# Splitting each weight's conversion around the H block of a slot

## The chip, the cores and the metric

The kernel runs on one core of a Trainium2 chip. The metric is the device time in microseconds of one execution. TensorE is called PE below, VectorE DVE, ScalarE ACT, GpSimd POOL and the queue that issues the transfers SP.

## The reference

Three computations follow each other:

```python
# attention: batch 4, 12 heads, 448 tokens, head size 64, causal
scores = q @ k.T / 8;  attn = exp(masked scores - row maximum);  attn /= row sum
x = (attn @ v) as [1792, 768]
# MLP: w_in [768, 2048], w_out [2048, 768], drawn as 64-bit floats
h = x @ w_in;  g = max(0.01 * h, h);  x = g @ w_out
# soft mixture: phi [768, 32], 8 experts of 4 slots, w1 [8, 768, 1024], w2 [8, 1024, 768]
logits = x @ phi;  d = softmax(logits, over tokens);  c = softmax(logits, over slots)
slot_input = d.T @ x;  slot_out[e] = max(slot_input[e] @ w1[e], 0) @ w2[e];  out = c @ slot_out
```

## The kernel before

**Attention** goes by pairs of heads: 24 pairs n, six to a batch. A pair takes three slots, which we call A, B and C after the first six pairs: A has the products of the probabilities of pair n-1 with v (tile `O`), their row sums (`dn`) and the transposed maxima (`mps`, copied to `mr`); B has score products of pair n+1 (`S`, for the row maxima on DVE, tiles `junk` and `mxe`), the transposed scores `T` of pair n for its first key block, and once more `S`; C has the two further `T`, one more `S` and the transposes of q and k (`qkps`, copied to `qkt` on ACT in line 349 and DVE in line 350). ACT makes the probabilities `P` of each `T` by an exponential (L408). The tiles `S` and `T` share two PSUM buffers in turn: the second `S` of B waits for the maxima of the first, and the `S` of C waits for the exponential of the first `T` of C. On DVE the reciprocals of the row sums (L450, after ACT's copy in L448) and the scaling of `O` (L483) stand in the same queue as the maxima.

**The MLP's first product** of batch b runs in the slots of batch b+1: one H block per slot, 18 products of 448 columns for 128 columns of w_in, evicted by ACT (L668, tile `g`). There are 18 slots to a stage and 16 blocks; the slots 6 and 15 have none. There is one PSUM buffer for H.

**The weights** come as 64-bit floats and are converted in the same slots, in units of 128 columns of w_in (`i`) or 128 rows of w_out (`o`, whole, or in two halves from o10 on). A unit's elementwise passes are: ACT takes magnitude and sign (L200, L201), DVE the unit's maximum (L203, w_in only) and the two passes that put the 32-bit float together (L204, L205), after which the next raw tile can be loaded. For w_in, a TensorE product (`w_ps`) and a chain of small DVE operations (L116 to L124) make a power-of-two scale `w_s` of the maximum; then ACT scales the sign (L221), POOL multiplies (L222), ACT makes the high half (L228) and POOL the low half (L229). For w_out, POOL multiplies (L238), and the products `wt_ps`, `wp_ps`, `wf_ps` with their copies on ACT (L253, L262, L266) fold it with phi. Units i0 to i5 are done during the first batch's attention, i6 to i15 in the slots of pairs 7 to 12, o0 to o9 in those of pairs 13 to 18, o10 to o15 in those of pairs 19 to 23.

**Order.** Each engine runs its queue in order. A scheduler sets the queues when the program is built, from the order in which the code emits the work and the data's dependences; what stands under `tc.high_priority` (attention and H blocks) is ranked as if it had been emitted 300 places earlier. Each unit is a generator whose `yield`s divide it into steps, and `prep_step` advances every running unit by one step per slot, behind attention and block.

Of the kernel before, what the change touches and what calls it, by code (L numbers as in the profile page):

```python
# [10 lines left out]
F32 = mybir.dt.float32  # L11
# [14 lines left out]
AHEAD = 300  # L26
EARLY = (6, 10, 10)


def as_float(bits):  # L30
    return struct.unpack("<f", struct.pack("<I", bits))[0]
# [3 lines left out]
def tile_attn_moe_softmoe(ctx: ExitStack, tc: tile.TileContext, q, k, v, w_in, w_out, phi, w1, w2, out, dbg=None):  # L35
    nc = tc.nc
# [6 lines left out]
    E, _, FE = w1.shape  # L43
# [3 lines left out]
    NP = H // 2  # L47
    NF = DFF // 128
# [9 lines left out]
    ident = const.tile([128, 128], F32, name="ident")  # L58
# [29 lines left out]
    def ps_tr(name, shape=(128, 512)):  # L88
        return psum.tile(list(shape), F32, tag="tr", bufs=TR[0], name=name)
# [16 lines left out]
    tr = partial(in_order, nc.tensor.transpose)  # L106


    def pow2_scale(absmax, name, shift=23, bias=0, out=None):


        ps = ps_tr(f"{name}_ps", (128, 128))
        op = nc.tensor.matmul if name == "v0" else mm
        op(ps, absmax.to_broadcast([128, 128]), ident, start=True, stop=True)
        m1 = const.tile([128, 1], F32, tag="p2_m1", bufs=2, name=f"{name}_m1")
        nc.vector.tensor_reduce(m1, ps, AX.X, ALU.max)  # L116
        nc.vector.tensor_scalar(m1, m1, as_float((27 + bias) << shift), None, ALU.max)
        e = const.tile([128, 1], I32, tag="p2_e", bufs=2, name=f"{name}_e")
        nc.vector.tensor_scalar(e, m1.bitcast(I32), shift, None, ALU.logical_shift_right)
        si = const.tile([128, 2], I32, tag="p2_s" + name[0], bufs=4, name=f"{name}_s")  # L120
        nc.vector.tensor_scalar(si[:, 0:1], e, -(2**23), (268 + bias) * 2**23, ALU.mult, ALU.add)
        if out is None:
            out = si[:, 1:2].bitcast(F32)
        nc.vector.tensor_scalar(out.bitcast(I32), e, 2**23, -(14 + bias) * 2**23, ALU.mult, ALU.add)  # L124
        return si.bitcast(F32)[:, 0:1], out
# [23 lines left out]
    for x, u in enumerate(units):  # L149
        stage = 0 if x < EARLY[0] else 1 if x < whole else 2  # L150
        order += [u + (h, stage) for h in ((0, 1) if stage == 2 else (None,))]
    waiting = list(order)
    pools = [None, None, None]
# [58 lines left out]
    def prep_in(u):  # L212

        f = u[1]
        am = const.tile([128, 1], F32, tag="w_am", bufs=2, name=f"w_am{f}")
        t, sg = to_f32(u, am)
        yield
        if f >= EARLY[0]:
            yield
        s_w, _ = pow2_scale(am, f"w{f}", 20, out=inv_w[:, f : f + 1])  # L220
        nc.scalar.activation(sg, sg, AF.Copy, scale=s_w)  # L221
        nc.gpsimd.tensor_tensor(t, t, sg, ALU.mult)  # L222
        w = t.rearrange("p (c f) -> p c f", c=NP)
        hi, lo = (w16[f // 4][:, x, :, 128 * (f % 4) : 128 * (f % 4 + 1)] for x in range(2))
        if f < EARLY[0] and f % 4 < HIP:
            nc.gpsimd.tensor_copy(hi, w)
        else:
            nc.scalar.copy(hi, w)  # L228
        nc.gpsimd.tensor_tensor(lo, w, hi, ALU.subtract)  # L229
        ready.add(u[:2])  # L230

    def prep_out(us):

        f, stage = us[0][1], us[0][3]
        wt = None
        for u in us:
            wo, sg = to_f32(u)
            nc.gpsimd.tensor_tensor(wo, wo, sg, ALU.mult)  # L238
            c0 = DH * (u[2] or 0)
            nc.sync.dma_start(  # L240
                wsc.rearrange("(k g a p) n -> k a g p n", k=4, g=4, a=4)[f // 4, f % 4][:, :, c0 : c0 + wo.shape[1]], wo
            )
            yield
            if u[2] is None:
                yield
            if wt is None:
                wt = pools[stage].tile([128, NP, 128], F32, tag="wt", bufs=1, name=f"wt{f}")
            for h in (0, 1) if u[2] is None else (u[2],):
                ps = ps_tr(f"wt_ps{f}_{h}", (128, 3, 128))
                for j in range(3):  # L250
                    c = 128 * (3 * h + j) - c0
                    tr(ps[:, j], wo[:, c : c + 128], ident)
                nc.scalar.copy(wt[:, 3 * h : 3 * h + 3], ps)  # L253
        yield
        psw = ps_tr(f"wp_ps{f}", (96, 128))
        for c in range(NP):
            j = c % 3
            mm(
                psw[32 * j : 32 * j + 32], phi_sb[:, c], wt[:, c], start=c < 3, stop=c >= 3, skip_group_check=True
            )  # L260
        w4 = pools[stage].tile([96, 128], F32, tag="w4", bufs=1, name=f"w4_{f}")
        nc.scalar.copy(w4, psw)  # L262
        yield
        psf = ps_tr(f"wf_ps{f}", (128, NS))
        mm(psf, w4, istack[:96, :NS], start=True, stop=True)
        nc.scalar.copy(wprime[:, f], psf)  # L266
        ready.add(us[0][:2])

    ready = set()

    started = [0]
    running = []

    def prep_step():

        for g in list(running):
            if next(g, 1) == 1:
                running.remove(g)

    def prep_start():  # L280
        u = units[started[0]]
        started[0] += 1
        us = [x for x in order if x[:2] == u]
        g = prep_in(us[0]) if u[0] == "i" else prep_out(us)
        next(g)
        running.append(g)

    def need(u):
        while u not in ready:
            if not running:  # L290
                prep_start()
            prep_step()

# [330 lines left out]
    def up(b, before=()):  # L626
# [14 lines left out]
        for f in range(NF):  # L641
            if b == 0:
                need(("i", f))
                scales(slice(f, f + 1))
# [134 lines left out]
    def stage(slots, count, columns_of_g=None):  # L779

        had = started[0]
        for x in range(slots):
            with tc.high_priority(offset=AHEAD):
                next(slots_of_attention, None)
                if columns_of_g is not None and x not in GAPS:
                    next(columns_of_g)
            prep_step()
            while started[0] < min(count, had + -(-(count - had) * (x + 1) // (slots - (4 if columns_of_g is None or count > NF else 6)))):
                prep_start()
        if columns_of_g is not None:  # L790
            with tc.high_priority(offset=AHEAD):
                for _ in columns_of_g:
                    pass
        while running:
            prep_step()

    if True:
        pools[0] = tc.alloc_tile_pool(name="conv1", bufs=1)
# [31 lines left out]
        slots = ["wg"] * (NG - 1) + ["wq"] * NQ + ["wx"] * NX + ["wg"] + ["wc"] * NC  # L830
# [78 lines left out]
        for c in range(4):  # L909
            wo = loaded.pop(("wo", c))  # L910
# [23 lines left out]
        for e in range(E):  # L934
            ph = ps2(f"ph{e}", (128, 256), tag="h", bufs=4)
            for hf in range(2):
                wt = loaded.pop(("w1", (e, hf)))
# [83 lines left out]
        for x, (t0, nt, c0, cols) in enumerate(pieces):  # L1021
            if x:
                load_next(1)
            wt = loaded.pop(("w2", x))
            hp = padded_h(t0 // 8)
            for h in (0, 1) if cols == DM else (c0 // DH,):
                for t in range(nt):
                    g = (t0 + t) % 4
# [19 lines left out]
GAPS = (6, 15)  # L1048
# [34 lines left out]
```

## Time and profile before

| | |
|---|---|
| median of 3 runs | 712.88 us (705.38, 712.88, 713.38) |
| the profiled execution | 705.66 us, of which the span of its instructions 703.9 us |
| PE busy | 592.6 us, 84% of the span |
| DVE, ACT, POOL busy | 358.0, 289.7, 236.6 us |
| mean granted TensorE clock | 0.951 |

The slots that the change touches lie between about 110 and 475 us of the span: the first H blocks run at 114 us, the third stage ends at about 475 us. Behind that the last batch's MLP follows, and then the experts' weights, which the transfers set. Times in the rows are microseconds from the span's start. An "idle before" of an engine is followed by what the profile takes as its releaser.

### The profile page before, as it was taken

Reading aid. Unit: us, or ns where it says so; the run is one execution under the profiler, and the core shown is the slowest. Engines: PE = TensorE matmul, PEld = TensorE weight load, DVE = VectorE, ACT = ScalarE, POOL = GpSimd, SP = SyncE. Lnnn points to the kernel's source line nnn. Section 1 sums busy time; section 2 is a strip of 40 time slices with the busy share of each in tenths; the row PEclk is TensorE's granted clock in tenths of the full one; section 3 lists DMA queues with packets and bytes.
Section 4 is the critical chain, followed back from the end, with each engine's and each line's share of the span. In section 5 each row is a group of like instructions: output and inputs, shape, how many; then the busy total and the mean of one; then the engine's idle time right before and its main releaser. Section 6 shows DMA issues by size and latency. Waiting matters only on the chain.

```text
span 703.9 us, 12298 instructions
## 1 busy us (share of the span) xinstructions
PE 592.6 (84%) x4836; PEld 334.8 (48%) x4836; DVE 358.0 (51%) x884; ACT 289.7 (41%) x571; POOL 236.6 (34%) x247
## 2 busy tenths in 40 slices
PE   3788868877989999899988979999997996998644
PEld 2555544544555555465555545554343443453114
DVE  5868646775764564654645655644555423001004
ACT  1577543656565356465444455442022112011013
POOL 4277743675586342553522434440000000000000
PEclk9999998997989999999999999999999997899798
DMA  9932352542643246663313422206979335999967
GB/s 182 270 99 49 70 173 54 169 129 85 167 145 109 66 150 170 178 189 112 97 49 111 109 81 64 79 24 230 303 279 406 107 146 219 426 423 425 423 259 313
DMA packets 102449, 125.67 MB, mean 179 GB/s; under 512 B 69240, under 2 KB 91256, under 8 KB 98296
## 3 DMA queue, kind: packets, MB, share of 16 engines
q1 hardware_dynamic: 102392, 124.89, 54.2%
q8 instruction: 38, 0.62, 0.4%
q14 instruction: 19, 0.16, 0.1%
HBM read 105.74 MB, written 19.14 MB: 177 GB/s over the span
## 4 chain that ended last, share of the span: by engine, by line
PE 48%; DMA 13%; DVE 11%; ACT 10%; POOL 8%; issue 7%; SPq 1%; ACTq 0%; DVEq 0%; POOLq 0%
PE H L102 22%; DMA w<-in_moe_w_dram 8%; PE O L102 5%; PE g_acc L102 3%; DVE g_nat L608 2%; DVE rs L450 2%; PE S L102 2%; ACT P L408 2%; PE qkps L102 2%; POOL cv_i_None L222 2%; PE ph L941 2%; DMA raw_i_None<-in_moe_w_in_dram 2%; PE dn L102 2%; PE L L102 2%; PE T L102 2%
## 5 line engine op out<-in xcount | busy, mean ns | idle before, releaser
L102 PE MATMUL H<-x,w 128*128 128x448 f16 x1152 | 234.8, 359 | 0.7 <-ACT g L668 0.7
L102 PEld LDWEIGHTS <-w 128*128 128x128 f16 x1152 | 112.5, 100 | 113.4 <-issue 22.5
L372 DVE CUSTOM_DVE_ANT_0 junk<-S,mask 112x224 bf16<-112x224 f32 (+3 forms) x192 | 85.1, 443 | 47.8 <-PE S L102 44.7
L668 ACT ACTIVATE g<-H,iv 128x448 f32<-128x448 f32 x58 | 36.7, 633 | 112.1 <-PE H L102 101.3
L450 DVE RECIPROCAL rs<-rs 128x224 f32<-128x224 f32 x36 | 53.4, 1524 | 38.2 <-ACT rs L448 38.2
L102 PE MATMUL S<-qkt 64*112 64x224 f32 (+3 forms) x192 | 33.8, 393 | 35.0 <-ACT P L408 21.8
L102 PE MATMUL O<-P,v 112*64 112x448 f32 (+3 forms) x384 | 57.4, 444 | 6.1 <-POOL P L412 4.4
L102 PE MATMUL T<-qkt 64*112 64x336 f32 (+3 forms) x576 | 58.4, 315 | 3.9 <-ACT P L408 3.2
L412 POOL TENSOR_SCALAR_AFFINE_SELECT P<-P 112x448 f32<-112x448 f32 x48 | 33.8, 708 | 82.1 <-ACT P L408 69.3
L408 ACT ACTIVATE P<-T 112x672 f32<-112x672 f32 (+1 forms) x72 | 55.8, 791 | 12.1 <-PE T L102 11.8
L485 POOL TENSOR_TENSOR x<-rs,x 128x448 f16<-128x448 f32 x24 | 25.3, 1053 | 84.9 <-ACT x L484 79.6
L102 PEld LDWEIGHTS T<-qkt 64*112 64x112 f32 x576 | 43.1, 180 | 10.4 <-ACT P L408 3.6
L421 POOL TENSOR_TENSOR tsum<-tsum,P 112x448 f32<-112x448 f32 (+1 forms) x48 | 46.4, 967 | 3.1
L102 PEld LDWEIGHTS O<-P,v 112*64 112x64 f32 x384 | 27.5, 148 | 35.2 <-issue 17.6
L1029 PE MATMUL po<-w,hz 128*32 128x384 f32 x256 | 27.3, 548 | 17.7 <-DMA w<-in_moe_w_dram 17.7
L417 POOL TENSOR_TENSOR tsum<-P 112x672 f32<-112x672 f32 x24 | 39.4, 1643 | 1.3
L102 PEld LDWEIGHTS S<-qkt 64*112 64x112 f32 x192 | 16.0, 184 | 50.1 <-ACT P L408 25.6
L933 POOL MEMSET hz<- 128x256 f32 x2 | 0.6, 312 | 109.6 <-PE g_acc L102 109.6
L608 DVE STREAM_TRANSPOSE g_nat<-g 128x448 f32<-128x448 f32 x26 | 16.5, 640 | 37.7 <-ACT g L668 37.7
L350 DVE TENSOR_TENSOR qkt<-qkps,qkt 128x448 fp32r<-128x448 f32 x48 | 28.9, 620 | 10.5 <-ACT qkt L349 10.5
L222 POOL TENSOR_TENSOR cv_i_None<-cv_i_None,cs_i_None 128x768 f32<-128x768 f32 x16 | 28.0, 1747 | 16.8 <-ACT cs_i_None L221 16.8
L384 ACT ACTIVATE mr<-mps,own 128x112 fp32r<-128x112 f32 x96 | 26.2, 361 | 16.0 <-PE mps L102 16.0
(174 smaller groups left out, 865.8 us busy)
## 6 DMA issues: line engine op xcount, KB each, us to landing
w<-in_moe_w_dram SPq DMA_DIRECT2D x32, 1536.0 KB, 20.8
raw_i_None<-in_moe_w_in_dram SPq DMA_DIRECT2D x16, 768.0 KB, 4.6
raw_o_None<-in_moe_w_out_dram SPq DMA_DIRECT2D x10, 768.0 KB, 6.0
g_far<-g SPq DMA_DIRECT2D x32, 224.0 KB, 6.4
gb<-g_far SPq DMA_DIRECT2D x8, 896.0 KB, 6.7
wo<-wsc SPq DMA_DIRECT2D x4, 1536.0 KB, 10.0
qk<-in_q_dram SPq DMA_DIRECT2D x48, 112.0 KB, 2.5
qk<-in_k_dram SPq DMA_DIRECT2D x48, 112.0 KB, 2.9
```

Of the source, the lines that this page charges most:

```text
L102: op(*args, **kwargs)
L222: nc.gpsimd.tensor_tensor(t, t, sg, ALU.mult)
L350: nc.vector.tensor_tensor(st[:, j, 1], p, st[:, j, 0].bitcast(F32), ALU.subtract)
L372: nc.vector.tensor_tensor_reduce(out=junk[:, :w], in0=ps[:, a, at : at + w], in1=mask[:, S - w :], scale=-1.0, scalar=3e38, op0=ALU.add, o ...
L408: nc.scalar.activation(x[:, :, o : o + at], ps[:, :, :at], AF.Exp, scale=SCALE)
L412: nc.gpsimd.affine_select(out=d, in_=d, compare_op=ALU.is_ge, fill=0.0, base=0, pattern=[[0, 4], [1, CP]], channel_multiplier=-1,)
L417: nc.gpsimd.tensor_tensor(tsum[:CP], p[0][:CP, :, 0, CP:], p[0][:CP, :, 1, : S - CP], ALU.add)
L421: nc.gpsimd.tensor_tensor(y, y, p[1][:CP, :, j, : S - CP * (j + 2)], ALU.add)
L450: nc.vector.reciprocal(rs[:, c : c + S // 2], rs[:, c : c + S // 2])
L608: nc.vector.transpose(g_nat[:, :, 32 * f : 32 * (f + n)].rearrange("p c (f x) -> p f c x", x=32), gts[b, f].rearrange("p (c x) -> p c x", ...
L668: nc.scalar.activation(g, ps, AF.Prelu, scale=iv[b][:, f : f + 1], alpha=SLOPE)
L1029: nc.tensor.matmul(po[h][32 * g : 32 * g + 32], hp[:, (t0 + t) % 8], wt[:, t, DH * h - c0 : DH * (h + 1) - c0], start=t0 + t < 4, stop=t0 ...
```

## The change

A unit's steps are now of two kinds. Steps that wait at `yield BEFORE` are emitted between a slot's attention products and its H block, steps that wait at `yield AFTER` behind the block. A new unit is started between attention and block too, so that its magnitude, sign and the DVE passes are emitted there; the scale's product, the transposes of w_out and the folding products come behind the block. For w_in the scale's product is emitted behind the block of the slot after the start (before: two slots after it, for f of 6 and more), and the passes that use the scale ahead of the next slot's block. For w_out the transposes move from the second to the first slot after the start, and of a unit in halves both halves are converted before the transposes. Nothing is added to or taken from the work.

```diff
 # prep_in
-        yield
-        if f >= EARLY[0]:
-            yield
+        yield AFTER
+        yield AFTER
         s_w, _ = pow2_scale(am, f"w{f}", 20, out=inv_w[:, f : f + 1])
+        yield BEFORE
         nc.scalar.activation(sg, sg, AF.Copy, scale=s_w)
 # prep_out
+            wos.append((wo, c0))
+            if u is not us[-1]:
+                yield BEFORE
+        if len(us) == 1:
+            yield AFTER
+        yield AFTER
...
-    def prep_step():
-        for g in list(running):
-            if next(g, 1) == 1:
-                running.remove(g)
+    def prep_step(phase):
+        for x in list(running):
+            if x[1] == phase:
+                x[1] = next(x[0], None)
+                if x[1] is None:
+                    running.remove(x)
...
 # stage
             with tc.high_priority(offset=AHEAD):
                 next(slots_of_attention, None)
-                if columns_of_g is not None and x not in GAPS:
-                    next(columns_of_g)
-            prep_step()
-            while started[0] < min(count, had + -(-(count - had) * (x + 1) // (slots - (...)))):
-                prep_start()
+            prep_step(BEFORE)
+            while started[0] < min(count, had + -(-(count - had) * (x + 1) // last)):
+                prep_start()
+            if columns_of_g is not None and x not in GAPS:
+                with tc.high_priority(offset=AHEAD):
+                    next(columns_of_g)
+            prep_step(AFTER)
```

What the scheduler makes of it, at three places. Up to pair 7 all queues are as before.

ACT at slots B and C of pair 10, from the H block's eviction `g0_8` on; `P0_448_144<-T10_1` is the exponential that the `S` of slot C waits for. First before, then now (lines behind 268 are 8 to 12 higher in the changed kernel):

```order
L668 ACTIVATE g0_8_2104<-H0_8_2085,iv0_1358 128x448
L484 CAST x16_1_1460<-rs9_2073 128x448
L408 ACTIVATE P0_448_144<-T10_0_2138 112x2x448
L221 ACTIVATE cs_i12_None_1932<-cs_i12_None_1932,w12_s_2114 128x768
L637 ACTIVATE iv0_1358<-inv_w_119,v0_s_269 128x1
L668 ACTIVATE g0_9_2175<-H0_9_2156,iv0_1358 128x448
L228 CAST w16_3_100<-cv_i12_None_1931 128x6x128
L200 ACTIVATE cv_i14_None_2122<-raw_i14_None_1881 128x768
L201 ACTIVATE cs_i14_None_2123<-raw_i14_None_1881 128x768
L221 ACTIVATE cs_i13_None_2051<-cs_i13_None_2051,w13_s_2185 128x768
```

```order
L676 ACTIVATE g0_8_2128<-H0_8_2109,iv0_1368 128x448
L416 ACTIVATE P0_448_144<-T10_0_2148 112x2x448
L492 CAST x16_1_1470<-rs9_2083 128x448
L221 ACTIVATE cs_i13_None_2028<-cs_i13_None_2028,w13_s_2138 128x768
L645 ACTIVATE iv0_1368<-inv_w_119,v0_s_269 128x1
L228 CAST w16_3_100<-cv_i13_None_2027 128x6x128
L200 ACTIVATE cv_i15_None_2170<-raw_i15_None_1915 128x768
L201 ACTIVATE cs_i15_None_2171<-raw_i15_None_1915 128x768
L676 ACTIVATE g0_9_2199<-H0_9_2180,iv0_1368 128x448
L416 ACTIVATE P0_448_144<-T10_1_2215 112x2x336
```

Before, four passes and an `iv` stand between `g0_9` and that exponential (its row follows the last one shown and one more `iv`); now three of them and the scaling L221 stand ahead of `g0_9`, each one unit further on.

DVE at slot C of pair 8, from the last two maxima of that slot on; L350 (now L358) frees the transposes' PSUM buffers:

```order
L372 ISA junk9_2_1_1772,mxe1_143<-S9_0_1761,mask_114 112x336
L372 ISA mxe1_143 112x1
L203 TENSOR_REDUCE w_am10_1715<-cv_i10_None_1716 128x1
L204 TENSOR_SCALAR cv_i10_None_1716<-cv_i10_None_1716 128x768
L350 TENSOR_TENSOR qkt10_1774<-qkps10_0_1775,qkt10_1774 128x448
```

```order
L205 SCALAR_TENSOR_TENSOR cv_i10_None_1693<-raw_i10_None_1435,cv_i10_None_1693 128x768
L380 ISA junk9_0_0_1776,mxe1_143<-S9_0_1771,mask_114 112x112
L380 ISA mxe1_143 112x1
L380 ISA junk9_0_1_1778,mxe1_143<-S9_0_1771,mask_114 112x112
L380 ISA mxe1_143 112x1
L380 ISA junk9_2_0_1780,mxe1_143<-S9_0_1771,mask_114 112x336
L380 ISA mxe1_143 112x1
L380 ISA junk9_2_1_1782,mxe1_143<-S9_0_1771,mask_114 112x336
L380 ISA mxe1_143 112x1
L358 TENSOR_TENSOR qkt10_1784<-qkps10_0_1785,qkt10_1784 128x448
```

The passes of unit i10 stood between the maxima and L350 and now stand ahead of the maxima.

DVE at slot B of pair 19, behind the reciprocals of pair 18; the second `S` of the slot (`S20_3`) waits for both maxima of `S20_1`:

```order
L372 ISA junk20_1_0_4172,mxe0_142<-S20_1_4169,mask_114 112x224
L372 ISA mxe0_142 112x1
L372 ISA junk20_1_1_4174,mxe0_142<-S20_1_4169,mask_114 112x224
L372 ISA mxe0_142 112x1
L608 STREAM_TRANSPOSE g_nat_4110<-g2_0_4157 128x14x32
L204 TENSOR_SCALAR cv_o10_0_4159<-cv_o10_0_4159 128x384
L205 SCALAR_TENSOR_TENSOR cv_o10_0_4159<-raw_o10_0_4106,cv_o10_0_4159 128x384
```

```order
L204 TENSOR_SCALAR cv_o10_0_4136<-cv_o10_0_4136 128x384
L380 ISA junk20_1_0_4172,mxe0_142<-S20_1_4169,mask_114 112x224
L380 ISA mxe0_142 112x1
L205 SCALAR_TENSOR_TENSOR cv_o10_0_4136<-raw_o10_0_4106,cv_o10_0_4136 128x384
L616 STREAM_TRANSPOSE g_nat_4110<-g2_0_4167 128x14x32
L380 ISA junk20_1_1_4174,mxe0_142<-S20_1_4169,mask_114 112x224
L380 ISA mxe0_142 112x1
```

The two conversion passes and the transposition of `g` stood behind the maxima and now stand ahead of the second one. In the same way L203 and L204 come ahead of the maxima in slot B of pair 7, and L204 and L205 in slot B of pairs 13, 16, 17, 20 and 22.

## Rows read from the trace of the kernel before

**Rows 1.** Busy time by stretch: stretch, length, PE, PEld, DVE, ACT, POOL, clock, DMA:

```profile
110.00:250.00 140.00, 120.62 (x789) 69.02 (x786) 89.64 (x223) 76.78 (x138) 75.41 (x58) 0.92 0.41 116
250.00:366.00 116.00, 106.73 (x856) 65.02 (x856) 62.38 (x144) 63.29 (x132) 47.39 (x41) 1.00 0.48 138
366.00:475.00 109.00, 101.43 (x781) 58.79 (x780) 61.74 (x143) 53.63 (x118) 43.65 (x47) 1.00 0.28 79
```

**Rows 2.** Waits of PE from 110 to 250 us: sum, times, longest:

```profile
PE S L102 <- ACT P L408: 13.0, 7, 3.0
PE w_ps L102 <- DVE qkt L350: 2.1, 1, 2.1
```

**Rows 3.** Waits of PE from 250 to 366 us:

```profile
PE S L102 <- DVE mxe L372: 3.1, 2, 1.6
PE S L102 <- ACT P L408: 2.2, 3, 1.3
```

**Rows 4.** Waits of PE from 366 to 475 us:

```profile
PE S L102 <- ACT P L408: 4.0, 3, 1.5
PE S L102 <- DVE mxe L372: 1.3, 2, 0.7
```

**Rows 5.** ACT's timeline, slot C of pair 10: start, duration, what, idle before:

```profile
195.04 0.83 ACT L228 CAST w<-cv_i_None 128x768 f16<-128x768 f32 x1
...
197.36 0.92 ACT L221 ACTIVATE cs_i_None<-cs_i_None,w_s 128x768 bf16<-128x768 bf16 x1
...
198.37 1.32 ACT L408 ACTIVATE P<-T 112x672 f32<-112x672 f32 x2
```

**Rows 6.** PE's timeline, the same slot:

```profile
199.12 0.81 PE L102 MATMUL S<-qkt 64*112 64x112 f32 x4 [3.00 <-ACT P L408]
...
201.41 5.55 PE L102 MATMUL H<-x,w 128*128 128x448 f16 x18
```

**Rows 7.** PE's timeline behind the H blocks of pairs 8 and 9:

```profile
155.91 0.49 PE L102 MATMUL w_ps<-ident,w_am 128*128 128x128 f32 x2 [2.13 <-DVE qkt L350]
156.33 2.76 PE L102 MATMUL O<-P,v 112*64 112x448 f32 x16
...
181.06 2.11 PE L102 MATMUL O<-P,v 112*64 112x448 f32 x16
```

**Rows 8.** DVE's timeline, pairs 7 to 10:

```profile
118.16 0.39 DVE L372 CUSTOM_DVE_ANT_0 junk<-S,mask 112x224 bf16<-112x224 f32 x1 [0.36 <-PE S L102]
...
131.02 0.29 DVE L116 TENSOR_REDUCE w_m<-w_ps 128x1 f32<-128x128 f32 x1 [0.56 <-PE w_ps L102]
...
137.32 0.90 DVE L203 TENSOR_REDUCE w_am<-cv_i_None 128x1 f32<-128x768 f32 x1
...
153.44 1.88 DVE L204 TENSOR_SCALAR cv_i_None<-cv_i_None 128x768 int32<-128x768 int32 x1
...
197.75 0.56 DVE L204 TENSOR_SCALAR cv_i_None<-cv_i_None 128x768 int32<-128x768 int32 x1
198.35 0.96 DVE L205 SCALAR_TENSOR_TENSOR cv_i_None<-raw_i_None,cv_i_None 128x768 int32<-128x768 int32 x1
```

**Rows 9.** POOL's timeline, slot C of pair 8:

```profile
153.26 1.65 POOL L229 TENSOR_TENSOR w<-cv_i_None,w 128x768 f16<-128x768 f32 x1
```

**Rows 10.** DVE's timeline, slot B of pairs 13, 16 and 17:

```profile
250.89 0.39 DVE L372 CUSTOM_DVE_ANT_0 junk<-S,mask 112x224 bf16<-112x224 f32 x1 [0.35 <-PE S L102]
...
316.40 0.39 DVE L372 CUSTOM_DVE_ANT_0 junk<-S,mask 112x224 bf16<-112x224 f32 x1 [0.90 <-PE S L102]
...
338.75 0.39 DVE L372 CUSTOM_DVE_ANT_0 junk<-S,mask 112x224 bf16<-112x224 f32 x1 [0.26 <-PE S L102]
```

**Rows 11.** DVE's timeline, slot B of pair 19:

```profile
379.24 0.64 DVE L608 STREAM_TRANSPOSE g_nat<-g 128x448 f32<-128x448 f32 x1
379.80 0.32 DVE L204 TENSOR_SCALAR cv_o<-cv_o 128x384 int32<-128x384 int32 x1
380.15 0.56 DVE L205 SCALAR_TENSOR_TENSOR cv_o<-raw_o,cv_o 128x384 int32<-128x384 int32 x1
```

More of the change, by code (lines that the diff above doesn't have):

```diff
@@ L234, in prep_out @@
         f, stage = us[0][1], us[0][3]
-        wt = None
+        wos = []
         for u in us:
@@ L242, in prep_out @@
             )
[L243 to L254, printed above, removed]
+            wos.append((wo, c0))
[4 more added lines that the diff above has]
+        yield AFTER
+        wt = pools[stage].tile([128, NP, 128], F32, tag="wt", bufs=1, name=f"wt{f}")
+        for h in (0, 1):
+            wo, c0 = wos[h % len(wos)]
+            ps = ps_tr(f"wt_ps{f}_{h}", (128, 3, 128))
+            for j in range(3):
+                c = 128 * (3 * h + j) - c0
+                tr(ps[:, j], wo[:, c : c + 128], ident)
+            nc.scalar.copy(wt[:, 3 * h : 3 * h + 3], ps)
+            if h == 0 and len(us) > 1:
+                yield AFTER
+        yield AFTER
         psw = ps_tr(f"wp_ps{f}", (96, 128))
@@ L262, in prep_out @@
         nc.scalar.copy(w4, psw)
-        yield
+        yield AFTER
         psf = ps_tr(f"wf_ps{f}", (128, NS))
@@ L269, in tile_attn_moe_softmoe @@
     ready = set()
+    BEFORE, AFTER = "before", "after"
     started = [0]
     running = []
-    def prep_step():
-        for g in list(running):
-            if next(g, 1) == 1:
-                running.remove(g)
+    def prep_step(phase):
[4 more added lines that the diff above has]
+                    running.remove(x)
     def prep_start():
@@ L284, in prep_start @@
         g = prep_in(us[0]) if u[0] == "i" else prep_out(us)
-        next(g)
-        running.append(g)
+        running.append([g, next(g)])
     def need(u):
@@ L781, in stage @@
         had = started[0]
+        last = slots - (6 if columns_of_g is not None and count <= NF else 4)
         for x in range(slots):
@@ L784, in stage @@
                 next(slots_of_attention, None)
-                if columns_of_g is not None and x not in GAPS:
+            prep_step(BEFORE)
+            while started[0] < min(count, had + -(-(count - had) * (x + 1) // last)):
+                prep_start()
+            if columns_of_g is not None and x not in GAPS:
+                with tc.high_priority(offset=AHEAD):
                     next(columns_of_g)
-            prep_step()
-            while started[0] < min(count, had + -(-(count - had) * (x + 1) // (slots - (4 if columns_of_g is None or count > NF else 6)))):
-                prep_start()
+            prep_step(AFTER)
         if columns_of_g is not None:
@@ L794, in stage @@
         while running:
-            prep_step()
+            prep_step(BEFORE)
+            prep_step(AFTER)
     if True:
```

## The prediction, made before the changed kernel had run

> **What bounds the kernel now.** The table of busy times by stretch comes first [rows 1]: in the three stages that the change touches (365 us) PE is busy for 120.6, 106.7 and 101.4 us of 140, 116 and 109, far ahead of the other engines. So PE sets the pace, and the most that a better order could give is PE's idle time, 19.4, 9.3 and 7.6 us, 36 us in all, and what the clock loses in the first stage, where the mean granted is 0.92 against 1.00 in the others. The waits of PE tell whom it stands for [rows 2 to 4]: the score products `S` wait for ACT's exponentials 13.0, 2.2 and 4.0 us (19.2 in all), for DVE's maxima 3.1 and 1.3 in the second and third stage; and once a `w_ps` waits 2.1 us for DVE's L350. The timeline of one slot C then shows why. On ACT the exponential starts at 198.37, behind L228 at 195.04 and three more passes, the last of them L221 at 197.36 [rows 5]; PE stands still for 3.00 us, and the H block behind it takes 5.55 us [rows 6]. I count such slots C at pairs 8, 9 and 10.
>
> **The change, part by part.** No work is added or removed, so every term is a wait that goes or comes. The sum is made for the profiled execution, 705.66 us.
>
> (a) *Slots C of pairs 8 to 10, ACT.* At pair 8 the queue is as before, one unit further on, so nothing moves. At pairs 9 and 10 the passes behind the eviction `g` go, and the naive gain is all of the wait but the own time of an L221: 3.00 - 0.92 = 2.1 us each [rows 5, 6]. I count on none of it. What now stands ahead of `g0_9` needs a scale and a product: the scale's chain shares DVE with L205 and the maxima until about 1.4 us into the H block, then L221 takes 0.92 [rows 5], POOL multiplies (as a POOL pass of this width, 1.65 [rows 9]), L228 takes 0.83 [rows 5] and L200 and L201, taken as long as L221, 0.9 each: 1.4 + 0.9 + 1.65 + 0.8 + 1.8 = 6.6 us, while a block at full clock is over in some 3.5. The 1.4 us are an estimate: one L205 of 0.96 [rows 8] and half as much for a maximum. So `g0_9` itself goes late by 3 us and the exponential behind it starts where it did, 7 to 8 us after the block's start. At pair 9 the scale of unit i11 waits behind DVE passes of two units, with the same result. The exponential's wait is exchanged for the scale's. Ends: 0, and -4.2 with 2 us of clock for each of the two blocks, -8.2. Taken: 0.
>
> (b) *Slot B of pair 7, DVE.* L203 and L204 come ahead of the maxima that release the second `S`: 0.90 + 0.56 [rows 8], less 0.36 that DVE stood idle there [rows 8]: +1.1. Ends 0 and +1.5.
>
> (c) *Slots C of pair 7 to B of pair 8.* Unit i7's scale chain (L116 on) now shares DVE with L203, L204 and L205 of i8: 0.90 + 0.56 + 0.96 = 2.4, less DVE's idle 0.56 [rows 8]: +1.9. Behind its L221 wait, in ACT's queue, L448's copy and `mr`; behind L448 the reciprocals, and behind these the maxima that the second `S` of pair 8 waits for. So it comes out on PE. Ends 0 and +2.4.
>
> (d) *End of pair 8, DVE.* The passes of i10 leave the place between the maxima and L350, where L204 took 1.88 us [rows 8]; PE's wait of 2.13 us for L350 goes [rows 7], and with it the `O` products that ran 2.76 instead of 2.11 us [rows 7]: -2.13 - 0.65 = -2.8. The `w_ps` that waits there is one unit further on but in the same place, so the gain is real unless another pass is late. Ends 0 and -4, if the row sums behind `O` recover too.
>
> (e) *Slots B of pairs 13, 16, 17, DVE.* L204 and L205 ahead of the maxima, 0.56 + 0.96 = 1.52 [rows 8] less the idle time that DVE had in front of these maxima, 0.35, 0.90 and 0.26 [rows 10]: 1.2 + 0.6 + 1.3 = 3.1. Of that PE covers some, because folding products of the next unit now stand ahead of the slot's `S` at pairs 16 and 17; I take +2.2. Ends 0 and +3.1.
>
> (f) *Slots B of pairs 19, 20, 22, DVE.* At 19, L204, L205 and the transposition of `g`: 0.32 + 0.56 + 0.64 = 1.5 [rows 11]; PE already waits for the maxima there (part of the 1.3 us of [rows 4]), so all of it comes on top. At 20 and 22 L204 and L205, 0.9 each [rows 11]. Sum +3.3, of which I take off 0.5 for L201s that wait for a load and no longer stand ahead of an exponential: +2.8. Ends 0 and +3.3.
>
> (g) *The rest costs nothing.* The folding products of w_out run one slot earlier in the second stage: the same products, done earlier and missed at the end of that stage, where pair 18's slot without a block has 0.6 us less of them to cover its wait; that lies within (e). In the third stage PE's order is unchanged. In slots C of pairs 13 to 15 an L200 ahead of the exponential becomes an L201, of about the same length; it must also wait for POOL's L238 to free its tile, which I take to be done. On SP the raw loads are issued up to one `g` store earlier; a load waits for DVE's L205, and the stores behind it feed a batch that is read in the last stage. If a store hung there, the ring of three `g` tiles would cover three slots.
>
> Sum: 0 + 1.1 + 1.9 - 2.8 + 2.2 + 2.8 = **+5.2 us**, 710.9 us for an execution like the profiled one. Of the four executions known (three runs and the profiled one) two lie at 705.4 and 705.7 and two at 712.9 and 713.4; the profiled one is 7.2 us below the median. The forecast stands in the middle of the two levels, 3.6 us above the profiled one: 710.9 + 3.6 = 714.5.
>
> One rule bears on (c) to (f). The row: an L204 that took 0.56 us at 197.75 took 1.88 at 153.44 [rows 8], where POOL's L229 had begun at 153.26 and took 1.65 [rows 9]; L204 ends 0.4 us after L229. The Trainium skill, page "SBUF — State Buffer", section "Who interferes with whom", says that DVE and GpSimd share one pair of ports as an exclusive lock, and that the second to issue waits until the first is done. By that rule the trace agrees, and it speaks against this change wherever the passes now meet POOL's: the sum would have 1.3 us more for each L204 so met. My sum has none, since in slots B POOL has little to do in the second and third stage (47.4 of 116 and 43.7 of 109 us busy [rows 1]).
>
> **The rivals.**
>
> *The cover works (faster).* The magnitudes, signs and scalings run while ACT stands idle under the blocks; then the 19.2 us of waits for exponentials [rows 2 to 4] shrink to a few and the slow blocks of the first stage go (5.55 instead of some 3.5 us [rows 6], four like it: 8 us). 705.7 - 15 - 8 = 683, 689 in the middle of the two levels. For it: ACT has 63 us free in the first stage [rows 1]. Against it: (a), the scale and POOL's product are not there in time. Between this and the forecast, a gain of 2 to 10 us stays within 2%.
>
> *The conversion's chain takes over DVE (slower).* In slots A and B ACT's row-sum copy L448 stands behind an L221 or L201 that waits, the reciprocals and maxima start late, and the second `S` of every slot B pays, not of the seven alone that I count. Place: 13 slots B with a running conversion (pairs 7 to 10, 13 to 17, 19 to 22). Price: L204 and L205, 1.52 us each [rows 8], 19.8 us: 725.5, and 729 in the middle. It decides from 10 slots on (15 us). For it: (c), and the lock above. Against it: at pairs 8 and 10 the queue between reciprocals and maxima has the same passes as before, and in the third stage each pass is half as long.
>
> The lock as a rival of its own: each L204 that meets a POOL pass pays 1.88 - 0.56 = 1.3 us [rows 8]. With the ten units of the first stage on PE's path that is 13 us, 728 us on top of the forecast. The page named above is where such a rule stands. Against it: two such L204 are in the first stage now, and only one of them stood in PE's way.
>
> *The change moves nothing.* ACT's and DVE's orders differ too much for that, but the waits may well add up to nothing: 705 to 713.
>
> **How the numbers follow.** Forecast (+2 to +9 us) 0.50; nothing or a small gain, within 2%, 0.30; faster as meant 0.09; DVE's chain 0.07; the lock 0.04. A measurement of this kernel can tell about 2% (14 us), as its runs lie 8 us apart. Faster 0.09, slower 0.11, within 2% 0.80. The likeliest case gives 714.5. The lower ends of all terms, without clock, give -4.2 - 4 = -8.2, 697.5; the upper ends 1.5 + 2.4 + 3.1 + 3.3 = +10.3, 716 at the lower level and 723.2 at the median. All ends do not fall together, so the range is 702 to 724: below it lie the faster rival and part of the small gains, above it the two slower ones.
>
> **What would show it.** (a) The third `S` of pairs 9 and 10 still waits over 2 us, now behind L221 or a late `g`. (b), (c) The second `S` in slot B of pairs 7 and 8 waits over 1 us, with an L203 between reciprocals and maxima. (d) No wait of `w_ps` for L350. (e), (f) PE's waits for `mxe` in the second and third stage grow from 4.4 to 7 us and more. It is wrong if PE's idle time in the first stage falls by more than 6 us, if the H blocks there all run at one clock, or if an L238 or L201 turns up as the releaser of long waits.

## The result, and the profile after

Over 20 runs of each kernel the median went from 707.5 us (703.4 to 714.6) to 712.6 us (708.3 to 715.7): ratio **1.007**, 95% interval 1.0043 to 1.0096, so 3.0 to 6.8 us slower. The forecast was 714.5 us, within 2%, with +5.2 us as its sum. The profiled execution of the changed kernel took 709.98 us (span 708.3), 4.4 us more in the span than the one of before. The sum came out; the sections below show that two of its terms did not, and that in the profiles their errors cancelled.

The busy times by stretch of the changed kernel, columns as in [rows 1]:

```profile
110.00:250.00 140.00, 120.78 (x795) 68.87 (x793) 89.24 (x223) 78.50 (x140) 70.24 (x58) 0.92 0.40 115
250.00:366.00 116.00, 107.81 (x871) 66.26 (x868) 63.84 (x151) 65.43 (x134) 48.61 (x43) 1.00 0.47 140
366.00:475.00 109.00, 97.92 (x722) 56.07 (x721) 59.47 (x135) 51.22 (x112) 38.22 (x43) 0.97 0.27 77
```

PE is as busy as before in the first stage, 1.1 us busier in the second, 3.5 us less in the third, and there the granted clock fell from 1.00 to 0.97. The starts of the H blocks say the same more sharply. The first block starts 1.13 us earlier than before, an offset that the change does not make. The last of the first stage (239.63, before 240.54) is 0.91 us early, so that stage cost 0.2 us; the last of the second (365.01, before 367.58) is 2.57 us early, a gain of 1.7; in the third the last four are 4.28 us late (473.36, before 469.08): this stage lost 6.9 us, and nothing behind it changes that.

PE's waits of the changed kernel, from 110 to 250 us, from 250 to 366 us, and from 366 to 475 us (to hold against [rows 2], [rows 3] and [rows 4]):

```profile
PE S L102 <- ACT P L416: 12.3, 6, 3.7
PE S L102 <- DVE mxe L380: 3.9, 4, 2.1
PE dn L102 <- POOL tsum L429: 1.8, 1, 1.8
```

```profile
PE S L102 <- ACT P L416: 3.0, 4, 1.1
PE S L102 <- DVE mxe L380: 2.3, 3, 1.2
```

```profile
PE S L102 <- DVE mxe L380: 4.6, 3, 1.8
PE S L102 <- ACT P L416: 4.5, 3, 2.0
```

In the first stage the waits for exponentials, which the change could have taken away, are nearly all there (13.0 before), the wait of `w_ps` is gone, and a wait for POOL's sums is new. In the second stage the waits for the maxima fell from 3.1 to 2.3 us. In the third stage the waits for the maxima grew from 1.3 to 4.6 us. PE's timeline of the changed kernel in that stage shows the rest of its loss:

```profile
423.20 4.92 PE L102 MATMUL H<-x,w 128*128 128x448 f16 x18
...
438.52 3.57 PE L102 MATMUL H<-x,w 128*128 128x448 f16 x18
...
445.31 0.45 PE L102 MATMUL S<-qkt 64*112 64x448 f32 x2 [1.80 <-DVE mxe L380]
445.70 5.26 PE L102 MATMUL H<-x,w 128*128 128x448 f16 x18
```

A block at the full clock takes 3.57 us; these two took 4.92 and 5.26, 3.0 us more. Of the 6.9 us lost, 3.9 are waits and 3.0 are these two blocks.

### The profile page after: what moved, and what is told of

Its sections match the earlier page's. It is cut to its first block, busy times and chain, and to the rows that moved or that the text cites. A ratio compares the mean times of both kernels' runs of the same rounds, so it can differ in the third digit from the quotient of the medians.

```text
span 708.3 us, 12312 instructions
## 1 busy us (share of the span) xinstructions
PE 592.1 (84%) x4836; PEld 334.2 (47%) x4836; DVE 358.7 (51%) x884; ACT 292.1 (41%) x571; POOL 230.9 (33%) x247
## 4 chain that ended last, share of the span: by engine, by line
PE 49%; DMA 14%; DVE 12%; POOL 8%; ACT 8%; issue 5%; SPq 2%; ACTq 0%; DVEq 0%; POOLq 0%
PE H L102 23%; DMA w<-in_moe_w_dram 8%; PE O L102 5%; DVE rs L458 3%; DMA raw_i_None<-in_moe_w_in_dram 3%; PE g_acc L102 3%; DMA raw_o<-in_moe_w_out_dram 2%; DVE g_nat L616 2%; PE S L102 2%; ACT P L416 2%; PE qkps L102 2%; PE dn L102 2%; PE T L102 2%; PE L L102 2%; PE ph L953 2%
## 5 line engine op out<-in xcount | busy, mean ns | idle before, releaser
L102 PE MATMUL H<-x,w 128*128 128x448 f16 x1152 | 240.3, 365 | 0.7 <-ACT g L676 0.7
L102 PEld LDWEIGHTS <-w 128*128 128x128 f16 x1152 | 114.0, 101 | 117.3 <-issue 29.3
L102 PE MATMUL O<-P,v 112*64 112x448 f32 (+3 forms) x384 | 54.5, 425 | 5.9 <-POOL P L420 4.4
L420 POOL TENSOR_SCALAR_AFFINE_SELECT P<-P 112x448 f32<-112x448 f32 x48 | 29.1, 609 | 85.4 <-ACT P L416 73.7
L358 DVE TENSOR_TENSOR qkt<-qkps,qkt 128x448 fp32r<-128x448 f32 x48 | 29.0, 621 | 12.4 <-ACT qkt L357 12.4
L102 PE MATMUL T<-mr,onesr 64*112 64x448 f32 (+1 forms) x192 | 30.6, 315 | 3.9 <-ACT mr L392 3.9
L222 POOL TENSOR_TENSOR cv_i_None<-cv_i_None,cs_i_None 128x768 f32<-128x768 f32 x16 | 27.2, 1700 | 17.5 <-ACT cs_i_None L221 17.5
```

The costliest lines, as they stand in the source:

```text
L102: op(*args, **kwargs)
L358: nc.vector.tensor_tensor(st[:, j, 1], p, st[:, j, 0].bitcast(F32), ALU.subtract)
L420: nc.gpsimd.affine_select(out=d, in_=d, compare_op=ALU.is_ge, fill=0.0, base=0, pattern=[[0, 4], [1, CP]], channel_multiplier=-1,)
```

## The experiments

The theories at the start: **D**, DVE's passes that now stand ahead of the maxima make the loss (terms b, c, e, f); **A**, ACT's queue does, through exponentials behind passes that wait (point a); **C**, the clock does, by itself. Each kernel below ran 6 to 12 times, in turn with the kernel before on the same chip. Its time is given as a ratio to the kernel before, with the 95% interval, since the chips differ by some us (medians of before: 707.25, 704.72 and 706.53 us in the three sittings).

**The three stages apart.** Each unit takes the new or the old steps, by the stage that it starts in:

```diff
+            new[0] = b in (1,)        # then (2,), then (3,)
...
-        g = prep_in(us[0]) if u[0] == "i" else prep_out(us)
+        if new[0]:
+            g = prep_in(us[0]) if u[0] == "i" else prep_out(us)
+        else:
+            g = old_in(us[0]) if u[0] == "i" else old_out(us)
```

> The new steps in the first stage alone (units i6 to o5), the second and third stage as before. The prediction's sum (its terms b, c, d): +0.2 us. What the two profiles show of this stage (the H block at 247 us starts as early against the first block as before, its slow blocks cost 2.4 us more and its waits 2.2 less): also about 0, between -2 and +2, with the w_ps wait for L358 gone and the third S of pairs 8 to 10 still waiting 3 us. The rival that slow blocks make the loss: +2 to +3. Seen as wrong for all of them: beyond 5 us either way.

> The new steps in the second stage alone. The prediction's term e: +2.2 us, from maxima that come late in slots B of pairs 13, 16 and 17. What the two profiles show: -1.5 us, of which the slot without a block at pair 18 gives about -2.3, because the folding products that stood there are done a slot earlier; the maxima of 13, 16 and 17 cost under 1 us together. If the first holds it is slower than the kernel before by 2 us, if the second it is 1 to 2 us faster.

> The new steps in the third stage alone. The prediction's term f: +2.8 us. The waits of the two profiles: +3.7 us (second S of slots B at pairs 19, 20 and 22 waits 0.7, 1.4 and 1.2 us longer for mxe, and 0.6 us at pair 19's slot C). If the two slow H blocks of that stage (4.92 and 5.26 us) follow from these waits: +6.7 us, with H blocks over 4.5 us again in 420 to 450 us. If the slow blocks came by themselves: +3 to +4 and no slow block in that stage.

Measured: first stage alone 0.9982 (0.9942 to 1.0021), second 0.9982 (0.9945 to 1.0019), third **1.0051** (1.0015 to 1.0088). Only the third stage costs something that can be told from nothing, 1.1 to 6.2 us. The forecast of the second stage (+2.2) lies outside its interval, -3.9 to +1.3 us; the -1.7 of the two profiles lies inside. The three middles add up to +0.15%, the whole change to +0.7%; the sum of three such intervals is wide enough for both. In the first kernel's profile not all is as it was expected: pair 9's third `S` waits 1.31 us, not 3, and a `w_ps` waits 1.3 us for DVE's copy of the transposes once more, behind pair 9's block instead of pair 8's. In the third kernel's profile three H blocks of the third stage are slow (4.73, 5.21 and 5.26 us), none of them between 420 and 450 us; whether they follow from the waits stays open.

On theory C the first kernel has an answer that was not asked for. Its second and third stage have the order of the kernel before, and yet its profile shows slow blocks there, at places where [rows 1] have a clock of 1.00:

```profile
359.61 5.70 PE L102 MATMUL H<-x,w 128*128 128x448 f16 x18
...
389.59 4.40 PE L102 MATMUL H<-x,w 128*128 128x448 f16 x18
...
412.28 4.99 PE L102 MATMUL H<-x,w 128*128 128x448 f16 x18
```

So a slow block in one profiled execution cannot be put down to the order of that execution. The waits can, where they come back.

**DVE's passes held behind the maxima**, in the changed kernel:

```diff
-        if absmax is not None:
+        with tc.issue_after(last_on(mybir.EngineType.DVE)) if stage in (1, 2) else ExitStack():
+            if absmax is not None:
...
```

> The changed kernel with one thing taken back: in all units from i6 on, DVE's passes L203, L204 and L205 are held behind the last DVE instruction of the slot's attention, so they no longer stand ahead of the slot's maxima; ACT's, POOL's and PE's places stay. If DVE's order makes the loss (terms b, c, e, f): the second S waits at pairs 19, 20 and 22 go back to under 0.7 us, and the time is 5 to 8 us under the changed kernel's 712.6, so 0 to 3 under the kernel before. If ACT's order or POOL makes it: within 2 us of the changed kernel. If DVE's passes held so late make the scale and the next load late: slower than the changed kernel by 3 us or more, with L201 waiting for loads.

Measured 0.993 (0.9889 to 0.997): under the kernel before, and 1.4% (10 us) under the change. But the place is not where D had it. In the third stage the waits for `mxe` are still 4.4 us: a unit starts in slot A, which has no maxima, and a pass held behind the last DVE work of that slot (the reciprocals) still stands ahead of the maxima of slot B. The gain is in the first stage. There the 17th block starts 127.1 us after the first one, 5.6 us earlier than before (132.7). In the two other profiles with these passes held (kernels further down) it starts 3.8 and 2.5 us earlier than before, and in the four profiles that have the new steps in this stage and hold nothing there, between 0.3 us earlier and 0.9 us later. The profiled execution as a whole took 707.72 us, among the slowest of its 12 runs (699.1 to 708.7), with two slow blocks in the third stage. Pair 9's third `S`, in the changed kernel and in this one:

```profile
173.57 0.81 PE L102 MATMUL S<-qkt 64*112 64x112 f32 x4 [2.98 <-ACT P L416]
...
175.86 5.71 PE L102 MATMUL H<-x,w 128*128 128x448 f16 x18
```

```profile
172.67 0.51 PE L102 MATMUL S<-qkt 64*112 64x112 f32 x4 [1.30 <-ACT P L417]
...
173.93 3.57 PE L102 MATMUL H<-x,w 128*128 128x448 f16 x18
```

That wait is for an exponential, on ACT. Its length alone shows little: with the new steps in the first stage alone, where nothing is held, it is as short, and in the last kernel below, which holds DVE's passes, it is 2.97 us. In both profiles with the short wait the block ahead of it took 5.26 us, and PE spent the time there. The line of the first stage alone:

```profile
173.16 0.50 PE L102 MATMUL S<-qkt 64*112 64x112 f32 x4 [1.31 <-ACT P L478]
```

What the hold moves is the start of what is waited for. The exponential stands behind ACT's scaling pass L221 (L222 here), and that pass waits for the scale, which comes from DVE:

```profile
170.88 0.94 ACT L222 ACTIVATE cs_i_None<-cs_i_None,w_s 128x768 bf16<-128x768 bf16 x1 [0.62 <-DVE w_s L121]
```

It starts 56.8 us after the first H block (114.06) here and in the last kernel below, 58.7 us after it in the changed kernel (171.79 after 113.13) and with the first stage alone; in the third profile with held passes it is 58.6, behind two slow blocks. So D and A are two ends of one chain.

**The scale's pass held behind the exponentials** tests the other end:

```diff
         yield BEFORE
-        nc.scalar.activation(sg, sg, AF.Copy, scale=s_w)
+        with tc.issue_after(last_on(mybir.EngineType.Activation)) if f >= EARLY[0] else ExitStack():
+            nc.scalar.activation(sg, sg, AF.Copy, scale=s_w)
```

> The changed kernel with ACT's scaling pass L221 (and so L228 behind it) held behind the slot's last exponential, for the units of the first stage; nothing else is taken back. If the exponentials of slots C wait behind an L221 that waits for its scale (the prediction's point a; the trace of the changed kernel shows L221 waiting 2.31 us for w_s ahead of the exponential at pair 9): the third S of pair 9 waits under 1 us instead of 2.98, and the time is 2 to 6 us under the changed kernel's 712.6 (the upper end with slow H blocks that go). If DVE's order makes those waits, and ACT's queue only passes them on: within 1.5 us of the changed kernel. If L221 and POOL's products come too late for the H blocks: slower by 2 us or more, with H waiting for w.

Measured 1.0011 (0.9977 to 1.0046), 0.6% or 4.2 us under the change. ACT's queue at pair 9, slot C, first in the changed kernel, then in this one (whose lines are one higher, L222 for L221):

```profile
171.79 0.94 ACT L221 ACTIVATE cs_i_None<-cs_i_None,w_s 128x768 bf16<-128x768 bf16 x1 [2.31 <-DVE w_s L121]
172.63 0.28 ACT L645 ACTIVATE iv<-inv_w,v_s 128x1 f32<-128x1 f32 x1
172.81 1.33 ACT L416 ACTIVATE P<-T 112x672 f32<-112x672 f32 x2
```

```profile
165.34 0.74 ACT L417 ACTIVATE P<-T 112x672 f32<-112x672 f32 x1 [0.38 <-PE T L102]
...
169.03 0.95 ACT L222 ACTIVATE cs_i_None<-cs_i_None,w_s 128x768 bf16<-128x768 bf16 x1
```

In the changed kernel the pass waits 2.31 us for its scale while the exponential stands behind it; moved behind, it holds nobody up, and the third `S` of pair 9 starts with no wait at all. The profiled execution, 699.83 us, is the fastest of the 12 (median 706.72).

**Both holds, with the third stage in its old order.** Two kernels: new steps in stages 1 and 2 with DVE's passes held there, and the same with L221 held as well.

> The new steps in the first and second stage with DVE's passes held behind the maxima in these two, and the third stage in the order of the kernel before. If the loss of the change is all in the third stage and the gain of the held DVE passes all in the first (H blocks 5.6 us earlier by 247 us there): 6 to 7 us under the kernel before, about 700 us. If what the held passes gained came from elsewhere, or the third stage's loss follows from earlier transfers and not from its own order: 703 us or more.

> As the kernel with the held DVE passes and the third stage as before, and also ACT's L221 held behind the slot's last exponential. If both holds take away different waits (DVE's maxima at slots B, exponentials at slots C): 2 to 4 us under that kernel, 696 to 698. If they take away the same waits: within 1 us of it, about 700.

Measured 0.9931 (0.9898 to 0.9964) and 0.9966 (0.9938 to 0.9994). The two holds do not add up, as the chain says, which they cut at two places. But with both the kernel is neither 2 to 4 us faster than with DVE's hold alone nor the same within 1 us; its middle is 2.5 us slower, and the intervals overlap. Nor do the profiles settle what each hold is worth. From the first H block to the 17th they show 132.7 us before, 127.1 to 130.2 with DVE's passes held, 123.0 with L221 held and 124.1 with both. There L221's hold is the larger one, by time it is the smaller (1.0011 against 0.993). This stays open.

The old third stage brought nothing that can be seen over the first kernel with held passes (0.9931 against 0.993), though the third stage alone costs 0.5%; the intervals are too wide to call this a contradiction, and it stays open.

**What makes the third stage's loss: DVE's passes cut short.** In the changed kernel:

```diff
+        z = slice(0, 8 if stage == 2 else w)
-        nc.vector.tensor_scalar(ti, ti, 3, None, ALU.logical_shift_left)
-        nc.vector.scalar_tensor_tensor(ti, lw, 29, ti, ALU.logical_shift_right, ALU.bitwise_or)
+        nc.vector.tensor_scalar(ti[:, z], ti[:, z], 3, None, ALU.logical_shift_left)
+        nc.vector.scalar_tensor_tensor(ti[:, z], lw[:, z], 29, ti[:, z], ...)
```

> The changed kernel with DVE's passes L204 and L205 cut to 8 of 384 columns for the units of the third stage (the other columns keep the magnitude alone, so w_out's rows from o10 on are not converted; the data play no part in the timing). If DVE's passes ahead of the maxima make the loss of the third stage (term f): the waits for mxe at pairs 19, 20 and 22 fall from 4.6 to under 2 us, and the time is 3 to 6 us under the changed kernel's 712.6. If the loss comes from ACT's L201 that wait for loads, or from the clock by itself: within 1.5 us of the changed kernel.

Measured 1.0094 (1.006 to 1.0129): no gain. Its waits of PE in the third stage:

```profile
PE S L102 <- ACT P L417: 8.0, 5, 2.7
PE S L102 <- DVE mxe L381: 1.1, 2, 0.7
```

The waits for the maxima went as expected, from 4.6 to 1.1 us, and those for exponentials grew by as much, from 4.5 to 8.0. So in this stage D falls as the whole cause: DVE's passes were the last to be waited for, but behind them stood something as late. ACT's own waits in that stretch, in the kernel before and in the changed one, give a suspect:

```profile
ACT cs_o L201 <- DMA raw_o<-in_moe_w_out_dram: 22.7, 12, 4.2
...
ACT rs L448 <- PE dn L102: 7.2, 4, 1.8
```

```profile
ACT cs_o L201 <- DMA raw_o<-in_moe_w_out_dram: 22.8, 11, 4.8
...
ACT rs L456 <- PE dn L102: 2.9, 2, 2.3
```

L201 waits for w_out's loads as long as before. What differs is who stands behind it. ACT's timeline of the changed kernel in slot C of pair 19 and slots A to B of pair 20:

```profile
384.49 0.54 ACT L201 ACTIVATE cs_o<-raw_o 128x384 bf16<-128x384 f32 x1 [1.67 <-DMA raw_o<-in_moe_w_out_dram]
384.94 1.33 ACT L416 ACTIVATE P<-T 112x672 f32<-112x672 f32 x2
...
394.23 0.55 ACT L201 ACTIVATE cs_o<-raw_o 128x384 bf16<-128x384 f32 x1 [2.66 <-DMA raw_o<-in_moe_w_out_dram]
394.68 0.52 ACT L456 COPY rs<-dn 128x448 f32<-128x448 f32 x1
```

In the first pair of rows the exponential starts as soon as the load's pass is through; in the second the copy of the row sums does, and with it the reciprocals and then the maxima on DVE. Before, the copy waited for PE's `dn` and for nothing else:

```profile
395.05 0.53 ACT L448 COPY rs<-dn 128x448 f32<-128x448 f32 x1 [1.72 <-PE dn L102]
```

**A third raw tile in the third stage**, in the changed kernel and, as the control, in the kernel before:

```diff
-    BUFS = ((3, 4, 2), (3, 3, 2), (2, 2, 2))
+    BUFS = ((3, 4, 2), (3, 3, 2), (3, 2, 2))
```

> The changed kernel with three instead of two raw tiles in the third stage, so that each load of w_out can be issued one half earlier. If ACT's L201, which wait 22.8 us for these loads and now stand directly ahead of the exponentials and of the copy L456 of the row sums, make the third stage's loss: L201's waits fall under 8 us in all, the third S of pair 19 waits under 1.2 us instead of 2.03, the reciprocals start earlier, and the time is 4 us or more under the changed kernel (ratio to the kernel before 1.001 or less instead of 1.007). If DVE's order alone makes it (term f): the waits for mxe stay at 4 to 5 us and the time within 1.5 us of the changed kernel. If only the clock differs: no change of the waits, within 1.5 us.

> The kernel before with the same third raw tile, as the control. If the loads matter only in the order of the changed kernel: within 1.5 us of the kernel before, though L201's 22.7 us of waits shrink as much. If they cost the kernel before as much: 3 us or more faster, and then the third tile says nothing on the change.

Measured 1.0005 (0.9979 to 1.0031) and 0.9997 (0.9968 to 1.0027). The control does not move by more than can be told (-2.3 to +1.9 us); the changed kernel loses its whole loss, 0.65% or 4.6 us. ACT's waits for the loads in its third stage, and PE's:

```profile
ACT cs_o L201 <- POOL cv_o L238: 13.7, 9, 3.8
...
ACT cs_o L201 <- DMA raw_o<-in_moe_w_out_dram: 2.0, 2, 1.5
```

```profile
PE S L102 <- DVE mxe L380: 3.1, 3, 1.6
PE S L102 <- ACT P L416: 1.0, 1, 1.0
```

The wait for loads fell from 22.8 to 2.0 us, and part of it came back as a wait for POOL's L238, so that L201 waits 15.7 us in all and not under 8. The exponentials' waits went from 4.5 to 1.0 us, the maxima's from 4.6 to 3.1; pair 19's third `S` has none, and the copy of the row sums at pair 20 waits for `dn` again (1.22 us). Over the third stage its H blocks now lose 0.5 us against the kernel before, not 6.9, although one of them took 5.05 us.

The other profiles agree. Counted from the start of the 33rd H block to that of the 48th, and with what slow blocks took over 3.57 us taken off, the five with the new third stage and two raw tiles are 3.8 to 4.8 us longer than before, the four others with the old third stage and two raw tiles 0.2 to 3.2 us, and this one is 1.0 us shorter. The order of the third stage costs what it does mostly because it puts passes that wait for a load ahead of work that PE waits for. The third tile is not without effect on the old order: in the control's profile the waits of `S` fall from 5.3 to 3.1 us (2.6 for `mxe`, 0.5 for exponentials), in the changed kernel from 9.1 to 4.1. What is left of the waits for `mxe` bounds DVE's own part: 1.8 us over the 1.3 of before, 0.5 over the control's.

**The gains together**: all three stages in the new steps, DVE's passes of the first two held, and the third raw tile.

> All three stages in the new steps, DVE's passes of the first two stages held behind the maxima, and the third raw tile: the pieces that gained so far together. If the loss of the third stage is gone with the third tile: as the kernel with the old third stage or better, ratio 0.990 to 0.993 (5 to 7 us under the kernel before). If the third tile doesn't help: 0.997 or more.

Measured 697.9 us, **0.9882** (0.9843 to 0.992) over six runs, 8.3 us under the kernel before: faster than both kernels. In this form the new order is faster than the old one. No run holds DVE's passes in the order of before, so how much of the 8.3 us needs the change is not shown.

## Why the prediction was right, and where it was not

The forecast and its range (702 to 724) held, with the reason given for it in part, and in part by luck. Its base of 709.3 us was 1.8 us above the 707.5 that 20 runs gave; that is nearly all of the 1.9 us between 714.5 and 712.6.

**(a), zero, was right, and by the mechanism named.** The third `S` of pairs 8, 9 and 10 wait 3.01, 2.98 and 3.70 us. Pair 9's exponential starts behind an L221 that waits 2.31 us for its scale, as the forecast said it would. At pair 10 the scaling pass, POOL's product and the `g` behind them are late one after the other:

```profile
193.73 0.94 ACT L221 ACTIVATE cs_i_None<-cs_i_None,w_s 128x768 bf16<-128x768 bf16 x1 [2.57 <-DVE w_s L121]
...
196.44 0.83 ACT L228 CAST w<-cv_i_None 128x768 f16<-128x768 f32 x1 [1.59 <-POOL cv_i_None L222]
...
198.74 0.62 ACT L676 ACTIVATE g<-H,iv 128x448 f32<-128x448 f32 x1
```

The H block that this `g` evicts was over at 194.54, so it came 4.2 us late where 3 had been worked out. The kernel with L221 held in all units of the stage was 4.2 us faster (0.6%; the two intervals just touch). The rival that the cover works fell on this (its 689 us should read 686 by its own sum, and the four slow blocks of the first stage lose 5.8 us, not 8; no bound rests on either); that nothing moves fell on the interval, which begins at 1.0043; DVE's chain in all 13 slots B would have cost four times as much as came.

**(b)**, +1.1: the second H block lost 0.7 us against the first. Right in kind, below its price: the second `S` of pair 7 waits 0.81 us for the maxima, not over 1 us.

**(c)**, +1.9: the price was right (a new wait of 1.82 us), the place was not. L221 in slot A of pair 8 starts at 134.14 instead of 131.91, 2.2 us later, behind L203 to L205 on DVE. But PE did not pay at pair 8's second `S`, which waits less than before (0.53 us against 1.46). It paid one slot earlier, for POOL's sums. PE's, POOL's and DVE's rows there:

```profile
134.43 0.79 PE L102 MATMUL dn<-tsum,onesr 128*64 128x336 f32 x4 [1.82 <-POOL tsum L429]
```

```profile
129.99 1.64 POOL L229 TENSOR_TENSOR w<-cv_i_None,w 128x768 f16<-128x768 f32 x1
131.60 2.77 POOL L429 TENSOR_TENSOR tsum<-tsum,P 112x448 f32<-112x448 f32 x2
```

```profile
130.69 1.36 DVE L204 TENSOR_SCALAR cv_i_None<-cv_i_None 128x768 int32<-128x768 int32 x1
...
132.09 1.77 DVE L205 SCALAR_TENSOR_TENSOR cv_i_None<-raw_i_None,cv_i_None 128x768 int32<-128x768 int32 x1
```

Conversion passes now stand among POOL's sums, and the sums and DVE's passes meet and slow down together: 2.77 us for the two sums (1.87 at 130.14 before), 1.36 instead of 0.56 for L204 and 1.77 instead of 0.96 for L205 [rows 8]. The Trainium skill, page "SBUF — State Buffer", section "Who interferes with whom", has DVE and GpSimd share a pair of ports, so that the one that comes second waits. These rows agree, both ways round. As a rival of its own (13 us) the rule fell: the first stage as a whole cost nothing.

**(d)**, -2.8: the wait of `w_ps` for L350 is gone, and `O` runs 2.11 instead of 2.76 us. From the sixth to the seventh H block the changed kernel makes up 2.1 us, although its sixth block is a slow one (5.25 us). PE's rows behind the eighth pair's last block, to hold against [rows 7]:

```profile
157.50 0.38 PE L102 MATMUL w_ps<-ident,w_am 128*128 128x128 f32 x2
157.81 2.11 PE L102 MATMUL O<-P,v 112*64 112x448 f32 x16
```

The first stage's terms summed to +0.2; measured +0.2 in the profiles and -1.3 us (-4.1 to +1.5) alone. That it is near zero is a balance of larger parts: in the profiles a single hold shortens the stage by 2.7 to 10.0 us.

**(e), the step that failed by its sign**: +2.2 was forecast for the second stage, -1.7 came. Slots B of pairs 13, 16 and 17 did lose 0.7, 0.2 and 0.7 us, 1.6 together. Only at pair 13 is that the maxima (a wait of 0.87 us); at 17 they make 0.20 us, at 16 nothing, and the rest is folding products that moved into these slots. Other slots gave it back (1.2 in slot C of pair 14, 1.0 in slot A of pair 17). What the forecast put at nothing in (g), pair 18's slot without a block, gave 2.4 us: the folding products that stood there (1.04 us of `wt_ps`, 0.64 of `wp_ps` and its wait of 0.58) are done a slot earlier, in time that PE stood idle. I had counted them only as cover that is missed.

**(f), the step that failed by its mechanism**: +2.8 was forecast, for L204 and L205 ahead of the maxima. The waits for maxima rose by 3.3 us, just as it said, and that was no proof: with the passes cut to 8 columns the time stayed. The main cause is ACT's L201, waiting for loads ahead of exponentials and of the row sums' copy. I had taken 0.5 us off for L201s that "no longer stand ahead of an exponential"; one now does. The prediction named a long wait behind an L201 as a sign that it would be wrong, and here it was.

So in the two profiles (e) was 3.9 us too high and (f), with the slow blocks, 4.1 too low, and the sum held by their cancelling. Over many runs the size of (f) is not refuted: the third stage alone cost 3.6 us (1.1 to 6.2), and 2.8 lies within that. The waits for `mxe` in the second and third stage were forecast to go from 4.4 to 7 us and went to 6.9, which looks like (e) and (f) confirmed and is not.

## What to carry to other kernels

A wait's releaser is the last link only: if its work is cut away and the time stays, another chain was as late, so shorten the suspect before believing it. Passes that wait for a transfer cost nothing where the work behind them has slack, and hold up the bounding engine where they are moved ahead of work that it needs; when passes are moved earlier, their loads have to come earlier too (here one more buffer). A product that leaves a slot in which the bounding engine is the last to finish is a gain, even if it looked like cover there.

## What the runs showed of the hardware that was not expected

The time of the very same program goes with the clock that the throttle granted. Of the 35 runs of the kernel before in the first of the three sittings, 20 had a mean granted clock of 0.944 to 0.956, and 19 of these took 703.9 to 707.9 us; 15 had 0.930 to 0.943, and 14 of these took 709.4 to 715.5. Nor does the wait ahead of a block decide alone: at pair 21 the second `S` waits 1.01 us before and after the change, and the H block behind it took 3.58 us in the one profile and 4.92 in the other:

```profile
422.69 0.45 PE L102 MATMUL S<-qkt 64*112 64x448 f32 x2 [1.01 <-ACT P L408]
423.07 3.58 PE L102 MATMUL H<-x,w 128*128 128x448 f16 x18
```

```profile
422.55 0.71 PE L102 MATMUL S<-qkt 64*112 64x448 f32 x2 [1.01 <-ACT P L416]
423.20 4.92 PE L102 MATMUL H<-x,w 128*128 128x448 f16 x18
```

A profile of one execution can thus hold 3 us of slow blocks that the order did not make, as large as the effects under study here.
